# A two-layer decode kernel: one step per K slot, 18 instead of 20 slots kept, and wider loads of V

## The chip, the cores and the metric

The kernel runs on one core of one Trainium2 chip. The metric is the device time of one execution in microseconds. Every execution does the whole computation, with all inputs in HBM at the start and the result in HBM at the end. The core has five engines with instruction queues of their own: TensorE (matrix multiplies and transposes into PSUM), VectorE, ScalarE, GpSimd and SyncE. Here SyncE issues every load. An engine runs its instructions in order; order between engines is made with semaphores.

## The reference

Two identical rounds of attention and MLP follow each other, with the same weights and the same caches in both. In bfloat16, with 8 batches, 32 query heads, 8 cache heads, 8192 cached positions and a head size of 128:

```python
x = A_x                                      # [8, 1, 512]
x = x + attention(layernorm(x))              # A_k_cache, A_v_cache, A_wq, A_wo
x = x + silu(layernorm(x) @ w1) @ w2
x = x + attention(layernorm(x))
x = x + silu(layernorm(x) @ w1) @ w2

# attention, per batch and cache head (4 query heads share one):
scores = q @ K.T * 128 ** -0.5               # K [8192, 128]
o = softmax(scores) @ V                      # V [8192, 128]; then o of all heads @ wo
```

One K cache head is 2 MB, and so is one V cache head. There are 64 pairs of a batch and a cache head, and each pair is needed in both layers: 268 MB of cache, which would be 537 MB if everything were loaded twice.

## The kernel before

**Tasks and slots.** A task is one pair of batch and cache head in one layer; there are 128 (`make_tasks`, line 147). K and V of a task are split into four granules of 512 KB. SBUF has an arena of 28 slots (`NSLOT`) of one granule each: 128 partitions of 4 KB. `KEEP = 20` says that the last 20 of a batch's 32 K granules are kept: they are loaded and transposed in layer 0 and stay in fixed slots until layer 1 of that batch has used them, so that layer 1 does not load or transpose them again. The other 8 slots, and kept slots between two uses, take the loads that stream through. Tasks come in rounds: five tasks of layer 0 whose K will be kept, then some five tasks that stream K, then five of layer 1 on kept K, and so on for the eight batches.

**Positions.** The program is written out by a loop over positions `p` (line 830). A position is half a granule (1024 cache rows); a task has eight. At an odd position a slot is complete. What is emitted at a position, in this order, is:

- the query block of the next task (`emit_q`), once a task;
- the transposes up to position `p + LT` with `LT = 2` (`emit_t`, line 503): eight 128x128 transposes of K by TensorE into one of three PSUM banks, and one copy back into the same place of the slot, on ScalarE for three of eight halves (`ACT_EVAC`, line 518) and on VectorE for the others (line 520);
- at odd `p`, the scores of the slot (`emit_s`, line 537, four matmuls of 512 columns), which need both copies of this slot, and then PV of the two positions that lie `LP = 12` behind (`emit_pv`, line 605, 16 matmuls);
- a stage of the softmax of the task before (`soft`, line 817): the maximum at position 0 of the next task, the shift (two passes of an f32 matmul, line 564, with two small VectorE operations) and the exponential on ScalarE (line 576) at position 1, the sums at 3, the transposes of P (line 592) at 4, the reciprocal at 7;
- a piece of the chain between the layers, if one is due: output projection (line 711), layer norm, MLP and the next query (line 693), cut into some two dozen pieces, one a position. VectorE and GpSimd do the layer norm (lines 639 to 682);
- `issue_until(p)` (line 473): the loads whose slot comes free at this position.

So the copies of a slot have a whole step (two positions) before its scores read them: while TensorE does scores and PV of one slot, the next one is already transposed.

**Loads.** `plan_loads` (line 188) decides before the program is written which load goes into which slot. Each load has a position `need` (for K: `i0 - LT`, where its transposes are emitted) and `after`, the last position that reads what lay in the slot. Loads are taken in the order of `need` and issued in that order by SyncE, one queue for all of them. For each load the planner takes the slot with the longest lead up to `ENOUGH`, by a clock with assumed times per position (`PACE`). V is tried four granules wide, then two, then one, and a width is taken where the lead by that clock is at least `EARLIEST`; streamed K is loaded one granule at a time, kept K four at a time.

Of the kernel before, what the change touches and what calls it, by code (L numbers as in the profile page):

```python
# [14 lines left out]
GPT = 8  # L15
GPG = 2
NSLOT = 28
KEEP = 20
LT = 2
PRE = 10  # L20
KWIDE = 1
VWIDE = 4
EARLIEST = {1: 0.0, 2: 9.0, 4: 14.0}
ENOUGH = 10.0
AHEAD = 10.0
PACE = (1.24, 0.64)
LP = 12
# [9 lines left out]
PVN = 12  # L37
CW = 32
SETTLE = 1
ACT_EVAC = (1, 4, 7)  # L40

BF16 = mybir.dt.bfloat16
FP32 = mybir.dt.float32
# [144 lines left out]
def plan_loads(tasks, kept, nslot, ngran):  # L188

    at = {t: i for i, t in enumerate(tasks)}  # L190
    homes = make_homes(kept, nslot, ngran)
    clock = [0.0]
    for layer, _b, g in tasks:
        for i in range(GPT):
            clock.append(clock[-1] + PACE[int(layer == 1 and (g, i // GPG) in kept)])
    clock += [clock[-1] + PACE[0] * (n + 1) for n in range(LP + GPT)]

    heap = []

    def push(kind, i, ks, home=None):  # L200
        layer, b, g = tasks[i]
        i0 = i * GPT + ks[0] * GPG
        if kind == "K":
            need = -1 if i0 < PRE else i0 - LT
            end = i if home is None else at[(1, b, g)]
            free = [end * GPT + (k + 1) * GPG - 1 for k in ks]
        else:
            need = i0 + GPG - 1 + LP
            free = [i * GPT + (k + 1) * GPG - 1 + LP for k in ks]
        heapq.heappush(heap, (need, kind, i, ks, Load(kind, i, b, g, ks, need, free, home)))  # L210

    def split(ks, width):
        return [ks[n:n + width] for n in range(0, len(ks), width)]

    reserved = [[] for _ in range(nslot)]
    for i, (layer, b, g) in enumerate(tasks):
        if layer == 0 and g in homes:
            ks, slot = homes[g]
            push("K", i, ks, slot)
            for n in range(len(ks)):  # L220
                reserved[slot + n].append(i * GPT + ks[0] * GPG - LT)
        for ks in split([k for k in range(ngran) if (g, k) not in kept], KWIDE):
            push("K", i, tuple(ks))
        for ks in split(list(range(ngran)), VWIDE):
            push("V", i, tuple(ks))

    def lead(need, after):
        return clock[max(0, need)] - clock[after] if after >= 0 else FAR

    free = [-2] * nslot  # L230
    loads = []
    while heap:
        d = heapq.heappop(heap)[-1]
        n = len(d.ks)
        if d.home is not None:
            for m in range(n):
                reserved[d.home + m].pop(0)
        else:
            best = None
            for slot in range(nslot - n + 1):  # L240
                held = free[slot:slot + n]
                if any(r and lead(r[0], f) < AHEAD for r, f in zip(reserved[slot:slot + n], d.free)):
                    continue
                after = max(held)
                waste = sum(clock[max(0, after)] - clock[max(0, f)] for f in held)
                key = (-min(lead(d.need, after), ENOUGH), waste, -after, slot)
                best = key if best is None else min(best, key)
            if n > 1 and (best is None or -best[0] < EARLIEST[n]):
                push(d.kind, d.task, d.ks[:n // 2])
                push(d.kind, d.task, d.ks[n // 2:])  # L250
                continue
            d.slot = best[-1]
        d.after = max(free[d.slot:d.slot + n])
        assert d.after < d.need or d.need == -1 and d.after == -2, (d.kind, d.need, d.after)
        free[d.slot:d.slot + n] = d.free
        loads.append(d)
    return loads

# [17 lines left out]
def _build(ctx, nc, A_x, A_k_cache, A_v_cache, A_wq, A_wo, B_w1, B_w2, out):  # L276
# [13 lines left out]
    kept = set(order[len(order) - KEEP:])  # L290
    tasks = make_tasks(B, HKV, (len(order) - KEEP) // NGRAN)
    assert len(tasks) == 2 * B * HKV
    task_at = {t: i for i, t in enumerate(tasks)}
    loads = plan_loads(tasks, kept, NSLOT, NGRAN)
    NG = len(tasks) * GPT
# [144 lines left out]
    with nc.Block() as block:  # L440

        @block.sync
        def _(sync_eng):
# [45 lines left out]
            load_rest()  # L489

            evacs = [0]
            tevacs = [0]
            tnext = [0]

            def has_t(i):
# [7 lines left out]
            def emit_t(i):  # L503
                b, g, k, h = where(i)
                slot = k_slot[(b, g, k)]
                n = tevacs[0]
                tevacs[0] += 1
                tb = evacs[0] % NTP
                evacs[0] += 1
                tpv = TPp[tb][:, :].rearrange("p (k q) -> p k q", q=128)  # L510
                steps = [
                    lambda c=c: pe.transpose(tpv[:, c, :], chunk(slot, h * GRP + c), ident[:, :])  # L512
                    for c in range(GRP)
                ]
                mm_group(steps, reads=[r_half(slot, h), "ident"], writes=[f"TP{tb}"])
                dst = half(slot, h)
                if n % 8 in ACT_EVAC:
                    op(act, lambda: act.copy(dst, TPp[tb][:, :]), reads=[f"TP{tb}"], writes=[r_half(slot, h)])  # L518
                else:
                    op(dve, lambda: dve.tensor_copy(dst, TPp[tb][:, :]), reads=[f"TP{tb}"], writes=[r_half(slot, h)])  # L520

            def emit_t_until(i):
                while tnext[0] <= min(i, NG - 1):
                    if has_t(tnext[0]):
                        emit_t(tnext[0])
                    tnext[0] += 1
# [10 lines left out]
            def emit_s(i):  # L537
                ti = i // GPT
                b, g, k, _h = where(i)
                slot = k_slot[(b, g, k)]  # L540
                bank, qn = ti % NSCP, ti % NQB
                steps = [
                    lambda c=c: pe.matmul(  # L543
                        SCp[bank][c * QUAD:(c + 1) * QUAD, :], QB[qn][:, NGRAN - 1 - k:NGRAN - 1 - k + QUAD],
                        ARENA[:, slot * SLOT + c * KB:slot * SLOT + (c + 1) * KB],
                        start=(k == 0), stop=(k == NGRAN - 1),
                    )
                    for c in range(NQ)
                ]
                mm_group(steps, reads=[r_half(slot, 0), r_half(slot, 1), f"QB{qn}"], writes=[f"SC{bank}"])  # L550
# [279 lines left out]
            for p in range(NG + LP + GPT + 1):  # L830
                tq = (p + LQ) // GPT
                if (p + LQ) % GPT == 0 and tq < ntask:
                    layer, b, _g = tasks[tq]
                    if layer == 1 and chain and chain_b[0] == b:
                        while chain:
                            chain.pop(0)()
                    emit_q(tq)
                emit_t_until(p + LT)
                if p % GPG == GPG - 1:
                    if p < NG:  # L840
                        emit_s(p)
                    for i in range(p - LP - GPG + 1, p - LP + 1):
                        if 0 <= i < NG:
                            emit_pv(i)
                ti, ph = p // GPT - 1, p % GPT
                if 0 <= ti < ntask and ph in soft:
                    for f in soft[ph]:
                        f(ti)
                if chain:
                    left = max(1, first1[chain_b[0]] - EARLY - p)  # L850
                    late = len(chain) <= QPARTS or len(chain) > left + QPARTS // 2
                    for _n in range(2 if late and len(chain) > left else 1):
                        chain.pop(0)()
                elif heads[turn[0]] and (p >= NG or turn[0] == B
                                         or p % GPG == GPG - 1 and (tasks[p // GPT][2], 0) in kept):
                    add_heads(turn[0])
                done = p - LP - GPT
                if done >= 0 and done % GPT == 0 and done // GPT < ntask:
                    tj = done // GPT
                    emit_norm(tj)  # L860
                    layer, b, _g = tasks[tj]
                    if layer == 0:
                        heads[b].append(_g)
                    elif b == B - 1:
                        heads[B].append(_g)
                    if layer == 0 and tj == last0[b]:
                        assert not chain and turn[0] == b
                        chain.extend([lambda b=b: add_heads(b)] * (HKV - summed[b]) + chain_of(b))
                        chain_b[0] = b
                        turn[0] = b + 1  # L870
                issue_until(p)
# [48 lines left out]
```

## Time and profile before

| | before |
|---|---|
| runs, median | 1208.91 us |
| runs, lowest to highest | 1202.98 to 1213.16 us |
| profiled execution: time, span | 1205.91 us, 1204.2 us |
| TensorE busy, weight loads busy | 975.9 us, 766.5 us |
| VectorE, ScalarE, GpSimd busy | 597.2, 374.0, 70.6 us |
| read from HBM, mean rate over the span | 465.05 MB, 386 GB/s |
| loads of V: 1 MB, 512 KB | 128, 256 |
| loads of K: 2 MB, 512 KB | 40, 192 |
| copies after the transposes: VectorE, ScalarE | 440 of 690 ns, 264 of 1009 ns |

Busy time is the time in which an engine had an instruction of the program running. The span runs from the first to the last instruction; the time of an execution is a little longer. A row of the timeline gives the start in us from the span's start, the duration in us, the engine, the line of the kernel, the operation and its operands (target, then sources); a bracket at its end is the engine's idle time before it and what ended that. The granted clock is the share of TensorE's full clock that the hardware let through.

### The profile page before, as it was taken

What the parts mean: (1) busy time and instruction counts of PE and PEld (TensorE: products, weight loads), DVE (VectorE), ACT (ScalarE), POOL (GpSimd) and SP (SyncE); (2) the same over time, 40 slices, a digit from 0 to 9 for tenths busy, and PEclk for the clock granted to TensorE, in tenths of its full rate; (3) what the DMA queues carried; (4) which work ended last, traced back from release to release, by engine and by line L of the source; (5) the groups of instructions that cost most, each with busy time, mean ns of one, the idle gap of its engine ahead of it and who ended that gap; (6) DMA issues with size and microseconds to landing.
All of it is one profiled execution on the core that took longest, in us unless ns stands there. A gap on an engine that the chain in (4) does not pass through costs nothing. (4 is left out here: it accounts for less than half of the span.)

```text
span 1204.2 us, 44647 instructions
## 1 busy us (share of the span) xinstructions
PE 975.9 (81%) x19960; PEld 766.5 (64%) x19960; DVE 597.2 (50%) x1830; ACT 374.0 (31%) x658; POOL 70.6 (6%) x172
## 2 busy tenths in 40 slices
PE   2788797888878897888878897888878887888885
PEld 2566675766656675677667675677566665767564
DVE  2345553556445553556445553556445544556444
ACT  1234331333133321443223322333133322333231
POOL 0000000000000000000000000000000000000000
PEclk9789999999999998999989998999989999999996
DMA  9999999999999999999999999999999999999994
GB/s 346 398 423 400 377 377 418 422 379 377 389 422 405 383 364 423 421 383 376 410 422 388 380 371 421 422 351 366 411 422 383 377 366 422 419 376 381 399 412 161
DMA packets 95903, 467.94 MB, mean 389 GB/s; under 512 B 9936, under 2 KB 15840, under 8 KB 73696
## 3 DMA queue, kind: packets, MB, share of 16 engines
q1 hardware_dynamic: 95712, 465.10, 97.7%
q8 instruction: 156, 2.56, 0.8%
q14 instruction: 35, 0.29, 0.1%
HBM read 465.05 MB, written 0.01 MB: 386 GB/s over the span
## 5 line engine op out<-in xcount | busy, mean ns | idle before, releaser
L520 DVE COPY arena<-TPp 128x1024 bf16<-128x1024 bf16 x440 | 303.4, 690 | 410.0 <-PE TPp L512 409.8
L512 PE MATMUL TPp<-ident,arena 128*128 128x128 bf16 x5632 | 412.7, 225 | 105.2 <-DMA arena<-in_A_k_cache_dram 88.3
L512 PEld LDWEIGHTS TPp<-ident,arena 128*128 128x128 bf16 x5632 | 342.4, 101 | 118.8 <-DMA arena<-in_A_k_cache_dram 98.3
L518 ACT COPY arena<-TPp 128x1024 bf16<-128x1024 bf16 x264 | 266.4, 1009 | 308.5 <-PE TPp L512 308.5
L616 PEld LDWEIGHTS OTp<-PT,arena 128*128 128x128 bf16 x8192 | 246.7, 97 | 169.3 <-issue 130.8
L616 PE MATMUL OTp<-PT,arena 128*128 128x48 bf16 x8192 | 301.6, 185 | 43.2 <-DMA arena<-in_A_v_cache_dram 16.8
L576 ACT ACTIVATE P<-SCp,small 128x512 bf16<-128x512 f32 x128 | 87.9, 687 | 467.7 <-DVE small L572 284.8
L543 PE MATMUL SCp<-arena,QB 128*32 128x512 bf16 x2048 | 210.7, 402 | 2.9 <-ACT QB L535 1.6
L584 POOL PARTITION_ALL_REDUCE small<-small x128 | 55.7, 435 | 947.1 <-DVE small L582 919.7
L554 DVE TENSOR_REDUCE small<-SCp 128x1 f32<-128x512 f32 x128 | 87.6, 684 | 39.9 <-PE SCp L543 39.5
L543 PEld LDWEIGHTS SCp<-arena,QB 128*32 128x32 bf16 x2048 | 53.1, 93 | 51.0 <-issue 5.1
L592 PE MATMUL TPp<-ident,P 128*128 128x128 bf16 x512 | 51.0, 223 | 33.1 <-ACT P L576 22.6
L564 PE MATMUL OTp<-P,small 128*128 128x64 f32 x256 | 54.4, 294 | 22.9 <-DVE P L556 22.2
L592 PEld LDWEIGHTS TPp<-ident,P 128*128 128x128 bf16 x512 | 30.8, 98 | 45.2 <-ACT P L576 26.6
L564 PEld LDWEIGHTS OTp<-P,small 128*128 128x128 f32 x256 | 38.3, 188 | 30.5 <-DVE P L556 28.9
L567 DVE SCALAR_TENSOR_TENSOR P<-OTp,small 128x64 f32<-128x64 f32 x128 | 36.3, 284 | 42.2 <-PE OTp L564 41.4
L582 DVE TENSOR_SCALAR small<-small 128x4 f32<-128x4 f32 x128 | 28.6, 223 | 36.7 <-ACT P L576 36.7
L596 DVE COPY PT<-TPp 128x256 bf16<-128x256 bf16 x128 | 36.9, 288 | 10.0 <-PE TPp L592 10.0
L711 PE MATMUL MISC<-at,wo 128*128 128x32 bf16 (+1 forms) x1152 | 39.8, 175 | 0.3 <-DVE at L630 0.3
L693 PE MATMUL MISC<-small,wq 128*128 128x32 bf16 x1024 | 35.0, 177 | 1.2 <-issue 1.2
L711 PEld LDWEIGHTS MISC<-at,wo 128*128 128x128 bf16 x1152 | 35.0, 96 | 0.4 <-DVE at L630 0.4
L556 DVE TENSOR_SCALAR P<-ident,small 128x64 f32<-128x64 bf16 x128 | 32.6, 254 | 4.5
(59 smaller groups left out, 300.4 us busy)
## 6 DMA issues: line engine op xcount, KB each, us to landing
arena<-in_A_v_cache_dram SPq DMA_DIRECT2D x128, 1024.0 KB, 10.4
arena<-in_A_v_cache_dram SPq DMA_DIRECT2D x256, 512.0 KB, 7.1
arena<-in_A_k_cache_dram SPq DMA_DIRECT2D x192, 512.0 KB, 7.7
arena<-in_A_k_cache_dram SPq DMA_DIRECT2D x40, 2048.0 KB, 14.7
wq<-in_A_wq_dram SPq DMA_DIRECT2D x1, 4096.0 KB, 16.8
wo<-in_A_wo_dram SPq DMA_DIRECT2D x1, 4096.0 KB, 29.6
w<-in_B_w_dram SPq DMA_DIRECT2D x2, 1792.0 KB, 25.2
P<-in_A_x_dram SPq DMA_DIRECT2D x1, 8.0 KB
```

Source lines behind the costliest of these rows:

```text
L512: lambda c=c: pe.transpose(tpv[:, c, :], chunk(slot, h * GRP + c), ident[:, :])
L518: op(act, lambda: act.copy(dst, TPp[tb][:, :]), reads=[f"TP{tb}"], writes=[r_half(slot, h)])
L520: op(dve, lambda: dve.tensor_copy(dst, TPp[tb][:, :]), reads=[f"TP{tb}"], writes=[r_half(slot, h)])
L543: lambda c=c: pe.matmul(SCp[bank][c * QUAD:(c + 1) * QUAD, :], QB[qn][:, NGRAN - 1 - k:NGRAN - 1 - k + QUAD], ARENA[:, slot * SLOT + c * K ...
L554: op(dve, lambda: dve.tensor_reduce(rowmax, SCp[bank][:, :], AX.X, ALU.max), reads=[f"SC{bank}"], writes=["rowmax"])
L564: mm_group([lambda: pe.matmul(every, ones.to_broadcast([128, 128]), spread, start=True, stop=True)], reads=["ones", "P"], writes=[f"OT{ob}"])
L576: op(act, lambda: act.activation(P[:, :], SCp[bank][:, :], ACT.Exp, bias=shift, scale=SM_SCALE, accum_out=rs[st]), reads=[f"SC{bank}", "sh ...
L584: op(pool, lambda: pool.partition_all_reduce(ssa[st], ssm[st], 128, bass.bass_isa.ReduceOp.add), reads=[f"ssm{st}"], writes=[f"ssa{st}"])
L592: lambda c=c: pe.transpose(tpv[:, c, :], P[:, c * 128:(c + 1) * 128], ident[:, :])
L596: op(dve, lambda: dve.tensor_copy(PT.rearrange("p x (c q) -> p x c q", q=USED), tpv.rearrange("p x (c q) -> p x c q", q=QUAD)[:, :, :, 0:U ...
L616: lambda c=c, cc=cc: pe.matmul(otp, chunk(slot, h * GRP + c), pv[:, cc % CPB, cc // CPB % NQ, k, :].unsqueeze(2).to_broadcast([128, REP, P ...
L711: lambda o=o, h=h: pe.matmul(MISC[:, o * w:(o + 1) * w], wo_sb[:, h, o * 128:(o + 1) * 128], rhs_of(h).to_broadcast([128, w]) if n == 1 el ...
```

## The change

- `KEEP` goes from 20 to 18: two K granules of one cache head per batch are no longer kept, so ten slots are left for streaming.
- `LT` is gone. At an odd position the transposes of both halves of the slot are emitted, then PV, then the scores of the same slot. A K load's `need` becomes the odd position of its slot.
- `ACT_EVAC` is gone: the first half of each slot is copied by ScalarE, the second by VectorE.
- The planner asks for more lead before it takes a double (12 instead of 9) or fourfold (16 instead of 14) load, counts lead up to 16 instead of 10, and, between slots that are otherwise equal, takes the one that held V last.

The loads become 240 single, 70 double and 33 fourfold for V, and 224 single, 8 double and 32 fourfold for K.

```diff
-KEEP = 20
-LT = 2
+KEEP = 18
...
-EARLIEST = {1: 0.0, 2: 9.0, 4: 14.0}
-ENOUGH = 10.0
+EARLIEST = {1: 0.0, 2: 12.0, 4: 16.0}
+ENOUGH = 16.0
...
-ACT_EVAC = (1, 4, 7)
...
-            need = -1 if i0 < PRE else i0 - LT
+            need = -1 if i0 < PRE else i0 + GPG - 1
...
-                reserved[slot + n].append(i * GPT + ks[0] * GPG - LT)
+                reserved[slot + n].append(i * GPT + (ks[0] + 1) * GPG - 1)
...
+    keys = [0] * nslot
...
-                key = (-min(lead(d.need, after), ENOUGH), waste, -after, slot)
+                key = (-min(lead(d.need, after), ENOUGH), waste, -after, sum(keys[slot:slot + n]), slot)
...
+        keys[d.slot:d.slot + n] = [int(d.kind == "K")] * n
...
-                if n % 8 in ACT_EVAC:
+                if h == 0:
                     op(act, lambda: act.copy(dst, TPp[tb][:, :]), reads=[f"TP{tb}"], writes=[r_half(slot, h)])
                 else:
                     op(dve, lambda: dve.tensor_copy(dst, TPp[tb][:, :]), reads=[f"TP{tb}"], writes=[r_half(slot, h)])
...
-                emit_t_until(p + LT)
                 if p % GPG == GPG - 1:
-                    if p < NG:
-                        emit_s(p)
+                    emit_t_until(p)
                     for i in range(p - LP - GPG + 1, p - LP + 1):
                         if 0 <= i < NG:
                             emit_pv(i)
+                    if p < NG:
+                        emit_s(p)
```

## The prediction

> **What bounds the kernel now.** I read the page first, then the waits, then single steps in the timeline.
>
> ```profile
> span 1204.2 us, 44647 instructions
> ...
> q1 hardware_dynamic: 95712, 465.10, 97.7%
> ```
> ```profile
> PE TPp L512 <- DMA arena<-in_A_k_cache_dram: 88.3, 85, 5.3
> ...
> PE OTp L616 <- DMA arena<-in_A_v_cache_dram: 16.8, 32, 1.4
> ```
>
> The first fence is from the page (span; the load queue's packets, MB and share), the second from the list of waits (us in total, times, longest). The load queue is busy for 97.7% of the span, so the loads look like the bound. But TensorE waited only 88.3 + 16.8 = 105 us for them, and the DMA share cannot separate the two: in windows of 30 us it is 1.01 where 421 GB/s move (480 to 510 us) and 0.99 where 374 GB/s move (540 to 570 us). I therefore asked how long a task (one cache head, four K slots) takes where nothing waits for a load. The exponential comes once per task, so the distance between two of them is a task's time.
>
> ```profile
> 262.93 0.69 ACT L576 ACTIVATE P<-SCp,small 128x512 bf16<-128x512 f32 x1 [3.00 <-DVE small L572]
> ...
> 271.30 0.69 ACT L576 ACTIVATE P<-SCp,small 128x512 bf16<-128x512 f32 x1 [3.00 <-DVE small L572]
> ```
>
> A task that transposes its K takes 8.37 us without load waits (262.93 to 271.30), 8.76 with one output-projection piece (254.17 to 262.93); a task on kept K takes about 4.9 (191.37 to 196.31). Tasks beside the MLP chain repeat 11.99 us in round after round (548.64 to 560.63). Loads at the best windows' 422 GB/s would need 4.19 MB / 422 = 9.9 us for a transposing task. So the two bounds are close: TensorE has 1.5 us of slack per transposing task, and that is what the change spends.
>
> ```profile
> 372.41 1.07 PE L512 MATMUL TPp<-ident,arena 128*128 128x128 bf16 x16 [0.93 <-DMA arena<-in_A_k_cache_dram]
> 373.07 0.69 DVE L520 COPY arena<-TPp 128x1024 bf16<-128x1024 bf16 x1 [2.87 <-PE TPp L512]
> 373.40 0.10 PEld L543 LDWEIGHTS SCp<-arena,QB 128*32 128x32 bf16 x4
> 373.41 0.40 PE L543 MATMUL SCp<-arena,QB 128*32 128x512 bf16 x4
> 373.51 1.01 ACT L518 COPY arena<-TPp 128x1024 bf16<-128x1024 bf16 x1 [2.12 <-PE TPp L512]
> ...
> 373.74 0.57 PE L616 MATMUL OTp<-PT,arena 128*128 128x48 bf16 x16
> ...
> 374.15 1.05 PE L512 MATMUL TPp<-ident,arena 128*128 128x128 bf16 x16
> ...
> 376.71 1.06 PE L512 MATMUL TPp<-ident,arena 128*128 128x128 bf16 x16
> ...
> 377.53 0.69 ACT L576 ACTIVATE P<-SCp,small 128x512 bf16<-128x512 f32 x1 [3.00 <-DVE small L572]
> ...
> 378.21 1.00 ACT L518 COPY arena<-TPp 128x1024 bf16<-128x1024 bf16 x1
> ```
>
> These are rows of the timeline (start, duration, engine, line). A step now is: transposes of the next slot (16 in 0.99 us to the next start), scores of the slot transposed a step earlier (0.33), PV (0.41): 1.73 us, nothing waiting. The copy of the first half starts 0.66 us after the transposes do, that of the second half at 1.10. In the third block the ScalarE copy starts only at 1.50, since the exponential stands ahead of it.
>
> **The change, part by part.**
>
> *Order within the step (LT gone, scores after PV).* The scores now need the copies of the transposes issued just before. First half on ScalarE: 0.66 + 1.01 = 1.67. Second half on VectorE: 1.10 + 0.69 = 1.79, plus 0.06 from a copy's end to TensorE: scores start at 1.85. PV covers only to 0.99 + 0.41 = 1.40. The step is 1.85 + 0.33 = 2.18 us. One step in four is worse: softmax_shift is emitted at the end of the task's first step, so its exponential is ahead of the next step's first-half copy on ScalarE; copy 1.50 to 2.50, scores at 2.56, step 2.89. With the two f32 matmuls of the shift (0.27) and the four transposes of P (0.23), a task is 3 x 2.18 + 2.89 + 0.50 = 9.93 us; the waits at L564 and L592 (0.39 and 0.22 a task) go, since transposes and PV now stand before them. Against 8.37: +1.56 on 88 tasks, **+137 us**. In the order of the built program 24 exponential steps have a chain or projection piece (16, 28 or 32 matmuls) before the transposes, which shortens the stall by 0.4 to 0.7: -12.
>
> *Tasks on kept K.* PV now precedes the scores, so the scores' 0.33 no longer covers the wait for PT: 32 tasks x 0.33 = +11.
>
> *KEEP 20 to 18.* Two slots a batch are loaded and transposed again in layer 1: 16 loads of 0.524 MB, 256 transposes, 32 copies. The eight tasks concerned go from 4.9 us to two stalled steps (2.18 + 0.27, 2.89) and two short ones (1.5 with the wait for PT, 0.7), 7.6: +22. The 8.4 MB at the mean 389 GB/s are 21.6 us of queue; I cost them at nothing, because the queue (473.5 MB, 1122 us at 422 GB/s) is then the shorter of the two, and keep the 21.6 as a rival.
>
> *ACT_EVAC gone.* ScalarE copies 368 halves instead of 264: +105 us busy, to some 479; VectorE loses 72 x 0.69 = 50. Both stay under half the span; their cost is in the steps above.
>
> *Layer-norm pieces.* Their chains (6 and 7 VectorE operations of some 0.19 us) sit ahead of the second-half copy. By counting through the new order I get about 2.4 us per batch against 1.31 now (a PV wait behind VectorE, once a round): +9, bounds 0 and +19.
>
> *Loads.* The plan asks for a slot ten positions (five steps) ahead of use instead of six or seven positions, from ten streaming slots instead of eight; V goes as 240 single, 70 double and 33 fourfold loads. TensorE being slower by 1.5 us a task, most of the 105 us of load waits go, and with them the slow clock behind the long ones:
>
> ```profile
> 208.07 1.89 PE L512 MATMUL TPp<-ident,arena 128*128 128x128 bf16 x16 [3.63 <-DMA arena<-in_A_k_cache_dram]
> ```
>
> Sixteen transposes took 1.89 us after that gap, 1.05 elsewhere; with the next block (1.81) and the scores some 2 us, eight times, 17. Of 122 I leave 26 standing: 9 at the start, where a fourfold V load and a third K load now go out ahead of the 7.9 MB of weights (2.6 MB, 6.5 us later for the K behind them), the rest where both bounds meet. Gain -96; bounds -122 and -40.
>
> Sum: 137 - 12 + 11 + 22 + 9 - 96 = +71. Span 1204.2 + 71 = 1275; the profiled execution took 1205.91, 1.7 more than its span, and 3.0 less than the median shown. I say **1276 us**. About 1% is what a measurement here tells from no change (the runs shown lie 0.8% apart).
>
> [...]
>
> **The rivals.**
>
> 1. *The queue stays the bound and hides the stalls* (for: 97.7%; a transposing task needs 9.9 us of loads anyway; against: 8.76 us tasks in the kept stage, 11.99 us tasks that no load explains). The cost is then the added bytes: 1204 + 21.6, **1227** us. Chance 0.10.
> 2. *Faster: the queue never runs dry.* With five steps of loads outstanding, everything moves at 422 GB/s: 1122 us, and about 27 for the edges (the last slice of 30 us moves 161 GB/s, the first 346), **1150**. It decides if transposing steps take under 2.48 us on average including the chain's pieces; against it stands that the copies' 1.85 us come from rows, and that PV is too short to cover them. Chance 0.08.
> 3. *They cancel:* the stalls cost half of what I count, the load waits go: about 1205. Chance 0.04.
> 4. *The clock falls.* Each transposing step now has a gap of 0.45 or 1.16 us. Gaps of 0.9 left the granted clock at 1.00 (510 to 540 us); a window behind a 3.6 us gap had 0.89 (600 to 630). At 0.89 throughout, 88 tasks of 7.4 us of matmul work take about 80 us more: **1355**. Chance 0.04. The Trainium skill (TensorE: Matmul & The Clock Gate, A second HAM failure mode) describes such an oscillation from short repeated gaps; no row here shows it.
>
> **How the numbers follow.** The forecast, 1235 to 1315 by its bounds, has 0.74. Range 1222 to 1312: it takes in rival 1 and leaves out 2, 3 and 4 and some of the upper end. Faster by over 1%: rival 2, 0.08; within 1%: 0.04; slower: 0.88.
>
> **What would show it.** Right: in a warm step the scores start 1.85 us after the transposes, 2.56 in the step with the exponential; idle time before the scores' matmuls (2.9 us now) becomes 150 to 220 us, ended by the copies; transposing tasks take 9.9 to 10.4 us; load waits at the transposes fall under 40 us; ScalarE is busy some 480 us. The eight long gaps before the first kept K go. Wrong: if the wait for K stays near 88 us, the queue still binds (rival 1); if the DMA rate stays above 410 GB/s in all stages, rival 2; if PEclk stands at 9 in most slices, rival 4. The term I trust least is the 26 us of load waits left.

## The result, and the profile after

The changed kernel takes 1300.49 us (median of 4 runs, 1298.46 to 1305.68), the kernel before 1211.04 us on the same chip: a ratio of 1.0758, 95% interval 1.0697 to 1.0819. The profiled execution took 1300.67 us with a span of 1298.8. The forecast was 1276 us, in a range of 1222 to 1312.

From the page of the kernel after: the span, the busy time of the engines, and the load queue with packets, MB and share.

```profile
span 1298.8 us, 45667 instructions
...
PE 978.0 (75%) x20216; PEld 801.4 (62%) x20216; DVE 574.2 (44%) x1758; ACT 478.2 (37%) x762; POOL 70.9 (5%) x172
...
q1 hardware_dynamic: 94416, 473.49, 94.2%
```

TensorE's matmuls are busy for 978.0 us, close to the 975.9 before. So nearly all of the 95 us that the span has gained are idle time of TensorE. The load queue still shows 94.2%, but its rate has fallen from 386 to 365 GB/s read. The list of waits of the kernel after (us in total, times, longest) says what TensorE waits for now:

```profile
PE SCp L540 <- DVE arena L517: 80.7, 173, 0.9
PE SCp L540 <- ACT arena L515: 73.2, 70, 1.1
PE SCp L540 <- DVE small L600: 33.5, 71, 0.5
...
PE TPp L509 <- DMA arena<-in_A_k_cache_dram: 7.4, 3, 6.4
```

The wait of the transposes for K has gone from 88.3 to 7.4 us, that of PV for V has left the list, and the scores' matmuls, which had 2.9 us of idle time in all, now have 229.1. These are their lines on the page, before and after (behind the second bar: the idle time before them, and what ended most of it):

```profile
L543 PE MATMUL SCp<-arena,QB 128*32 128x512 bf16 x2048 | 210.7, 402 | 2.9 <-ACT QB L535 1.6
```
```profile
L540 PE MATMUL SCp<-arena,QB 128*32 128x512 bf16 x2048 | 213.9, 406 | 229.1 <-DVE arena L517 80.7
```

(L600 in the list of waits is a small VectorE instruction that is emitted behind the copy; the scores read nothing of it and wait for the copy.) A transposing task without a projection piece, from one exponential to the next, in the timeline:

```profile
380.01 0.69 ACT L573 ACTIVATE P<-SCp,small 128x512 bf16<-128x512 f32 x1 [1.65 <-DVE small L569]
...
390.17 0.69 ACT L573 ACTIVATE P<-SCp,small 128x512 bf16<-128x512 f32 x1 [1.65 <-DVE small L569]
```

It takes 10.16 us, task after task, against 8.37 before (10.56 against 8.76 with a projection piece). And the steps themselves, first the one with the exponential, then one without:

```profile
410.52 1.06 PE L509 MATMUL TPp<-ident,arena 128*128 128x128 bf16 x16
...
411.29 0.69 ACT L573 ACTIVATE P<-SCp,small 128x512 bf16<-128x512 f32 x1 [1.65 <-DVE small L569]
411.41 0.56 PE L613 MATMUL OTp<-PT,arena 128*128 128x48 bf16 x16
411.61 0.69 DVE L517 COPY arena<-TPp 128x1024 bf16<-128x1024 bf16 x1 [0.35 <-PE TPp L509]
...
411.97 1.00 ACT L515 COPY arena<-TPp 128x1024 bf16<-128x1024 bf16 x1
...
413.02 0.40 PE L540 MATMUL SCp<-arena,QB 128*32 128x512 bf16 x4 [1.05 <-ACT arena L515]
...
416.27 1.05 PE L509 MATMUL TPp<-ident,arena 128*128 128x128 bf16 x16
416.91 1.01 ACT L515 COPY arena<-TPp 128x1024 bf16<-128x1024 bf16 x1 [1.56 <-PE TPp L509]
417.16 0.56 PE L613 MATMUL OTp<-PT,arena 128*128 128x48 bf16 x16
417.36 0.69 DVE L517 COPY arena<-TPp 128x1024 bf16<-128x1024 bf16 x1 [1.99 <-PE TPp L509]
...
418.20 0.40 PE L540 MATMUL SCp<-arena,QB 128*32 128x512 bf16 x4 [0.47 <-DVE small L600]
```

Transposes, PV, a gap, scores. With the exponential the scores start 2.51 us after the transposes (median of 70 such steps), right behind ScalarE's copy (411.97 + 1.00, and 0.05). Without it they start 1.93 us after them, though the last copy ends at 418.05: 0.15 us lie between its end and the scores. The prediction had 0.06 there, in every step.

### The profile page after: what moved, and what is told of

It reads as the page before. It is cut to its first block, busy times and chain, and to the rows that moved or that the text cites. A ratio compares the mean times of both kernels' runs of the same rounds, so it can differ in the third digit from the quotient of the medians.

```text
span 1298.8 us, 45667 instructions
## 1 busy us (share of the span) xinstructions
PE 978.0 (75%) x20216; PEld 801.4 (62%) x20216; DVE 574.2 (44%) x1758; ACT 478.2 (37%) x762; POOL 70.9 (5%) x172
## 3 DMA queue, kind: packets, MB, share of 16 engines
q1 hardware_dynamic: 94416, 473.49, 94.2%
## 5 line engine op out<-in xcount | busy, mean ns | idle before, releaser
L515 ACT COPY arena<-TPp 128x1024 bf16<-128x1024 bf16 x368 | 371.6, 1010 | 437.3 <-PE TPp L509 437.1
L509 PE MATMUL TPp<-ident,arena 128*128 128x128 bf16 x5888 | 405.5, 224 | 20.7 <-DVE arena L517 11.3
L509 PEld LDWEIGHTS TPp<-ident,arena 128*128 128x128 bf16 x5888 | 355.3, 101 | 50.6 <-issue 41.2
L540 PE MATMUL SCp<-arena,QB 128*32 128x512 bf16 x2048 | 213.9, 406 | 229.1 <-DVE arena L517 80.7
L517 DVE COPY arena<-TPp 128x1024 bf16<-128x1024 bf16 x368 | 254.4, 692 | 277.1 <-PE TPp L509 276.5
L613 PE MATMUL OTp<-PT,arena 128*128 128x48 bf16 x8192 | 298.3, 185 | 21.2 <-DVE at L627 14.7
L613 PEld LDWEIGHTS OTp<-PT,arena 128*128 128x128 bf16 x8192 | 265.6, 98 | 44.8 <-issue 44.5
L540 PEld LDWEIGHTS SCp<-arena,QB 128*32 128x32 bf16 x2048 | 61.6, 94 | 267.9 <-ACT arena L515 194.3
L564 DVE SCALAR_TENSOR_TENSOR P<-OTp,small 128x64 f32<-128x64 f32 x128 | 36.3, 284 | 109.7 <-PE OTp L561 109.7
L589 PE MATMUL TPp<-ident,P 128*128 128x128 bf16 x512 | 52.1, 226 | 19.3 <-ACT P L573 19.3
L561 PEld LDWEIGHTS OTp<-P,small 128*128 128x128 f32 x256 | 38.7, 190 | 39.6 <-issue 22.0
L561 PE MATMUL OTp<-P,small 128*128 128x64 f32 x256 | 56.5, 303 | 7.6 <-DVE P L553 7.6
L589 PEld LDWEIGHTS TPp<-ident,P 128*128 128x128 bf16 x512 | 29.8, 99 | 47.7 <-ACT P L573 27.2
L690 PEld LDWEIGHTS MISC<-small,wq 128*128 128x128 bf16 x1024 | 29.5, 96 | 7.2 <-issue 7.2
```

The source lines that it names most:

```text
L540: lambda c=c: pe.matmul(SCp[bank][c * QUAD:(c + 1) * QUAD, :], QB[qn][:, NGRAN - 1 - k:NGRAN - 1 - k + QUAD], ARENA[:, slot * SLOT + c * K ...
L561: mm_group([lambda: pe.matmul(every, ones.to_broadcast([128, 128]), spread, start=True, stop=True)], reads=["ones", "P"], writes=[f"OT{ob}"])
L589: lambda c=c: pe.transpose(tpv[:, c, :], P[:, c * 128:(c + 1) * 128], ident[:, :])
L613: lambda c=c, cc=cc: pe.matmul(otp, chunk(slot, h * GRP + c), pv[:, cc % CPB, cc // CPB % NQ, k, :].unsqueeze(2).to_broadcast([128, REP, P ...
```

## The experiments

### Where the time goes: the order of the step alone, and all but the order

`order_back` keeps every part of the change (18 kept, the copies by half, the planner's limits) but the order of the step. `order_alone` is the kernel before with the new order and nothing else.

```diff
 order_back, against after
+                emit_t_until(p + LT)
                 if p % GPG == GPG - 1:
-                    emit_t_until(p)
+                    if p < NG:
+                        emit_s(p)
                     for i in range(p - LP - GPG + 1, p - LP + 1):
                         if 0 <= i < NG:
                             emit_pv(i)
-                    if p < NG:
-                        emit_s(p)
```

(With it, K's `need` is `i0 - LT` again; `order_alone` makes the opposite edits in the kernel before. As `need` moves, the planner, itself unchanged, arrives at a somewhat different plan: in `order_alone` V goes as 202 single and 155 double loads.)

> The changed kernel with one part undone: transposes again two positions ahead, scores before PV, need of a K load as before. 18 slots kept, the planner's new limits and the copies by half stay. Step theory (the scores now wait for the copies of the same step, and that is the loss): idle time before the scores falls from 229 us to under 15, transposing tasks fall from 10.2 to 8.4 to 9.9 us, the time to 1185 to 1230. Rival, queue theory (8.4 MB more and the new sizes of loads are the loss): the time stays above 1270.

> The kernel before with the new order alone: transposes, PV, scores in one step. 20 slots kept, the old planner, the old copies (three of eight halves on ScalarE, so three slots of four have their last copy later than in the changed kernel, by some 0.2 us). Step theory: transposing tasks of 10.2 to 11.2 us, 1275 to 1330. Queue theory: the bytes are those of before, so 1200 to 1225.

Measured: `order_back` 1204.44 us, ratio 0.9936 (0.9913 to 0.9959); `order_alone` 1308.10 us, ratio 1.0800 (1.0758 to 1.0841). The waits of `order_back`:

```profile
PE TPp L510 <- DMA arena<-in_A_k_cache_dram: 97.8, 69, 10.8
...
PE OTp L614 <- DMA arena<-in_A_v_cache_dram: 13.4, 19, 3.3
```

and those of `order_alone`:

```profile
PE SCp L543 <- ACT arena L518: 127.9, 166, 1.2
PE SCp L543 <- DVE arena L520: 98.6, 164, 2.6
...
PE TPp L512 <- DMA arena<-in_A_k_cache_dram: 6.4, 3, 4.4
```

The two lists have changed places. (The fastest transposing tasks of `order_back` take 7.75 us, less than the 8.4 expected; the copies by half do that, as shown below.) With the old order TensorE waits for loads as before, whatever the planner and the slots; with the new order it waits for the copies, and the loads are mostly early though there are only eight streaming slots and the old planner (PV still waits 10.7 us for V there, against 16.8 before). So the order is the whole loss, and it also is what takes the load waits away: not because loads come earlier, but because TensorE comes later. The other parts together are worth 0.6% in the other direction.

### How long TensorE takes where no load is late

`half_v_after` and `half_v_before` leave out half of V's bytes (every load of V after the first into its slot brings only the first half of each granule) and keep the instructions of the engines.

```diff
+        if d.kind == "V" and all(d.slot + m in filled for m in range(n)):
+            src = src.rearrange("p (m c) -> p m c", c=SLOT)[:, :, 0:SLOT // 2]
+            dst = dst.rearrange("p (m c) -> p m c", c=SLOT)[:, :, 0:SLOT // 2]
+        filled.update(range(d.slot, d.slot + n))
```

> The changed kernel, which leaves out half of V's bytes: every load of V after the first into its slot brings only the first half of each granule, so some 130 of 473 MB are not loaded; all instructions of the engines stay. Step theory: TensorE's own pace binds, transposing tasks stay at 10.2 and 10.6 us, the time at 1280 to 1300. Queue theory: the time falls under 1200, by up to the 130 MB / 367 GB/s = 350 us.

> The kernel before, which leaves out half of V's bytes in the same way. This measures how much of its time is waiting for loads. Step theory: TensorE's pace comes to light, transposing tasks of 8.4 to 8.8 us throughout, the 105 us of load waits and the slow clock behind them go, 1080 to 1110. Queue theory: 335 MB at 389 GB/s are 860 us, so the time falls under 1050.

The page of `half_v_after`, and then that of `half_v_before`:

```profile
span 1293.3 us, 45667 instructions
...
q1 hardware_dynamic: 114512, 343.46, 77.0%
```
```profile
span 1090.3 us, 44647 instructions
...
q1 hardware_dynamic: 111072, 335.08, 86.1%
```

The times are 1295.10 and 1092.07 us, both where the step theory put them. Taking away 130 MB of loads saves the kernel after 1298.8 - 1293.3 = 5.5 us and the kernel before 1204.2 - 1090.3 = 113.9 us. Each is one run, and four runs of the kernel after lie 7 us apart: the 113.9 stands far out of that, the 5.5 says only that little is left. This splits the result as the prediction's sum did: TensorE's own pace became 1293.3 - 1090.3 = 203 us longer, and 113.9 - 5.5 = 108 us of load waits went. The net is 95, as in the two profiled executions (1298.8 - 1204.2). The split is good to some 10 us, for a few load waits are left in both kernels (first `half_v_before`, then `half_v_after`):

```profile
PE TPp L517 <- DMA arena<-in_A_k_cache_dram: 18.0, 16, 5.8
```
```profile
PE TPp L514 <- DMA arena<-in_A_k_cache_dram: 10.7, 2, 10.3
```

### Two terms of the step: the exponential ahead of the copy, and the hand-off to the scores

In `exp_late` the exponential is emitted two positions later, behind the next step's copies.

```diff
-            soft = {0: [softmax_max], 1: [softmax_shift, softmax_exp], 3: [softmax_sum], 4: [emit_pt], 7: [softmax_rcp]}
+            soft = {0: [softmax_max], 1: [softmax_shift], 3: [softmax_exp, softmax_sum], 4: [emit_pt], 7: [softmax_rcp]}
```

> The changed kernel with the exponential emitted after the transposes, PV and scores of position 3 instead of at position 1, so that on ScalarE it stands behind the copy of that step and not ahead of it. Step theory: the scores of that step start 1.93 us after the transposes, as in the other steps, instead of 2.50; the exponential then ends some 2.4 us after them and the transposes of P wait some 0.15; a transposing task falls from 10.16 to 9.7 to 9.8 us, the time to 1260 to 1275. Rival: the later exponential makes the transposes of P and PV late by as much as the scores gain, 1292 to 1305.

Measured: 1280.21 us (1275.31 to 1289.08), ratio 1.0559 (1.0503 to 1.0615). Nearly all transposing steps (321 of 368) now have their scores 1.93 us after the transposes, those with the exponential too, and a task takes 9.71 us, 0.45 less than in after: the mechanism holds. The time missed the expected range by 5 us. Two things that took part of the gain back are seen in the trace: the step that a chain piece had shortened is no longer shortened (in after 326.1 - 314.2 = 11.9 us for such a task, here 12.7), and loads are late again in some tasks (waits for K 18.2 instead of 7.4 us).

Next, the 0.15 us behind the copy. In the trace of after it is 146 ns in 292 steps in which VectorE's copy ends last, and 53 ns in 70 steps with the exponential, in which ScalarE's does. TensorE has two waits there, first for ScalarE's copy, then for VectorE's. `swap_waits` emits them in the other order and changes nothing else.

```diff
-                mm_group(steps, reads=[r_half(slot, 0), r_half(slot, 1), f"QB{qn}"], writes=[f"SC{bank}"])
+                mm_group(steps, reads=[r_half(slot, 1), r_half(slot, 0), f"QB{qn}"], writes=[f"SC{bank}"])
```

> The kernel after with one edit: the scores' two waits are emitted in the other order, first for VectorE's copy (which ends last in the steps without the exponential), then for ScalarE's. In the trace of after the scores follow the end of the last copy by 146 ns where the copy waited for second ends last (295 steps), and by 53 ns where the copy waited for first does (69 steps with the exponential). Theory, that the order of the two waits makes the difference: 146 falls to some 55 ns in the steps without the exponential and rises to some 146 in those with it, the scores of a plain step start 1.84 us after its transposes (the 1.85 of the prediction), a transposing task takes 9.95 to 10.0 us, and the time is about 1283 us. Rival, that the 146 ns belong to VectorE's end, whatever the order of the waits: the scores stay at 1.93, tasks at 10.16, and the time at 1300.

From the timeline of `swap_waits`, a step without the exponential:

```profile
413.35 1.05 PE L509 MATMUL TPp<-ident,arena 128*128 128x128 bf16 x16
414.00 1.01 ACT L515 COPY arena<-TPp 128x1024 bf16<-128x1024 bf16 x1 [1.47 <-PE TPp L509]
414.44 0.69 DVE L517 COPY arena<-TPp 128x1024 bf16<-128x1024 bf16 x1 [1.89 <-PE TPp L509]
...
415.19 0.40 PE L540 MATMUL SCp<-arena,QB 128*32 128x512 bf16 x4 [0.38 <-DVE arena L517]
```

The copy ends at 415.13, the scores follow after 55 ns (279 of the 299 steps in which VectorE's copy is last), 1.85 us after the transposes. With the exponential, where ScalarE's copy is last, it is now 145 ns (68 of 69 steps). The two numbers have changed sides with the order of the waits, so the engine that ends last is not the cause. A task takes 9.98 us instead of 10.16. The time is 1294.18 us (1288.92 to 1301.43), ratio 1.0693 (1.0627 to 1.0759); its interval overlaps that of after, so the gain of 0.18 us a task is shown by the steps and not by the times of the runs. The median is 11 us above the 1283 expected, the profiled execution (1290.31) 7.

`exp_late_swap` has both edits.

> The kernel after with both edits: the exponential two positions later (as in exp_late) and the scores' two waits in the other order (as in swap_waits). All 368 hand-offs then have VectorE's copy last and waited for first: scores 1.85 us after the transposes in every step, a transposing task 9.35 to 9.4 us. Theory, that TensorE's order alone sets the time: 365 steps by 0.09 us are 33 us less than exp_late's 1280, 1247 us, with load waits at the transposes near exp_late's 18 us. Rival, that the load queue takes its bound back as soon as a transposing task falls under the 9.9 us that its 4.19 MB need at 422 GB/s: load waits at the transposes rise to over 35 us and the time is 1255 to 1270 us, still slower than before.

Measured: 1262.48 us (1258.89 to 1264.62), ratio 1.0425 (1.0390 to 1.0460). From its timeline, the step with the exponential:

```profile
411.74 1.06 PE L509 MATMUL TPp<-ident,arena 128*128 128x128 bf16 x16
413.30 0.69 ACT L573 ACTIVATE P<-SCp,small 128x512 bf16<-128x512 f32 x1
413.58 0.40 PE L540 MATMUL SCp<-arena,QB 128*32 128x512 bf16 x4 [0.38 <-DVE arena L517]
414.13 0.40 PE L589 MATMUL TPp<-ident,P 128*128 128x128 bf16 x4 [0.16 <-ACT P L573]
```

The scores start 1.84 us after the transposes in 316 of 368 steps, and a task takes 9.44 us. Neither theory is wholly right. The time lies in the rival's range, but its reason is absent: the waits for K are 18.8 us, as in `exp_late`. The span fell by 15 us (1274.4 to 1259.4) instead of 33. Of the rest, some 10 are the wait for P at L589, 0.16 us in the last row (19.7 us in all in `exp_late`, 30.0 here), and 7 are tasks on kept K, which ran at a slower clock (204.7 us for the 32 of them there, 212.1 here; the last section has the rows). With both stalls shortened, the new order is still 4% slower than the kernel before.

### The other parts in the old order

Five kernels keep the old order and vary what is left. The first three start from `order_back`.

```diff
 back_keep20, against order_back
-KEEP = 18
+KEEP = 20
 back_old_copies, against order_back
-                if h == 0:
+                if n % 8 in ACT_EVAC:
 back_old_plan, against order_back
-EARLIEST = {1: 0.0, 2: 12.0, 4: 16.0}
-ENOUGH = 16.0
+EARLIEST = {1: 0.0, 2: 9.0, 4: 14.0}
+ENOUGH = 10.0
-                key = (-min(lead(d.need, after), ENOUGH), waste, -after, sum(keys[slot:slot + n]), slot)
+                key = (-min(lead(d.need, after), ENOUGH), waste, -after, slot)
 copies_alone, against before
-                if n % 8 in ACT_EVAC:
+                if h == 0:
 keep16, against back_old_plan
-KEEP = 18
+KEEP = 16
```

> The run order_back (1204.4 us) with 20 slots kept again, so that of the change the planner's limits and the copies by half stay. Queue theory for this order (load queue at 97.6%): 8.4 MB less at 394 GB/s are 21 us, 1180 to 1190. Rival: the two streaming slots that go cost in waits what the bytes save, 1200 to 1215.

> The run order_back with the old division of the copies (three of eight halves on ScalarE). The fastest transposing tasks go from 7.75 us back to 8.37. If the load queue binds wherever no chain runs, 1204 to 1212; if TensorE's pace binds, 88 times 0.6 us more, 1230 to 1255.

> The run order_back with the planner's old limits and tie break, so V goes as 158 single and 177 double loads instead of 248 single, 70 double and 31 fourfold. If the sizes and leads of loads matter, slower, 1215 to 1235; if not, 1198 to 1210.

> The kernel before with one edit: the first half of each slot is copied by ScalarE, the second by VectorE. Theory, that the order of the steps is the whole cost and that the copies by half are worth a few us in the old order (back_old_copies against order_back, 5 us): 1202 to 1210 us, and a transposing task without load waits some 7.8 instead of 8.4 us, since the exponential's copies no longer fall in an uneven pattern. Rival, that ScalarE, with a copy in every step, is late for the exponential: tasks over 8.4 us, 1220 us.

> The old order of a step and the old planner, copies by half, and two more slots for streaming (16 kept, 12 streaming) than in back_old_plan: 8 MB more to load and 16 more slots to transpose. If streaming slots are still worth more than their bytes (20 to 18 kept was worth 8 us with the other planner): 1195 to 1200 us. If the queue's bytes decide by now (8.4 MB at some 400 GB/s are 21 us): 1215 to 1225 us.

| kernel | kept | planner | copies | us, median | ratio, 95% interval |
|---|---|---|---|---|---|
| order_back | 18 | new | by half | 1204.44 | 0.9936 (0.9913 to 0.9959) |
| back_keep20 | 20 | new | by half | 1212.47 | 1.0003 (0.9971 to 1.0035) |
| back_old_copies | 18 | new | old | 1209.52 | 0.9975 (0.9955 to 0.9995) |
| back_old_plan | 18 | old | by half | 1203.83 | 0.9915 (0.9884 to 0.9947) |
| copies_alone | 20 | old | by half | 1201.99 | 0.9921 (0.9891 to 0.9950) |
| keep16 | 16 | old | by half | 1207.64 | 0.9987 (0.9962 to 1.0012) |

The copies by half are worth 0.4% with the new planner and 18 kept (0.9936 against 0.9975; the two intervals touch) and 0.8% alone, which is all that any of these kernels gains. In the old order a transposing task without load waits falls from 8.37 to 7.75 us with them: the wait at L564, 22.2 us in all before, is gone. In the profiled execution of `copies_alone` most of that came back as load waits, for K (103.6 us, 88.3 before) and for V (19.5, 16.8 before). The new limits of the planner cost 0.8% with 20 kept (`back_keep20` against `copies_alone`) and nothing with 18. Keeping 18 instead of 20 is worth 8 us only with the new limits; with the old ones (`copies_alone`, `back_old_plan`) the two are equal. Read alone, `order_back` against `back_keep20` would have credited the two streaming slots with those 8 us. `back_keep20` lies in its rival's range: 8.4 MB less to load gained nothing. `keep16` came out between its two expectations. `copies_alone` and `back_old_plan` are both faster than the kernel before, by 0.8%, and much faster than after.

## Why the prediction was right, and which terms were off

**The likeliest case happened, by its mechanism.** The bound moved from the load queue to TensorE's order, and the step's end is set by the copies. The time, 1300, lies 24 us above the forecast and inside the range. Nearly all that the prediction asked to see is there: idle time before the scores 229 us, ended by the copies (150 to 220 were named, so it is slightly over); transposing tasks 10.16 us, and 10.56 with a projection piece (9.9 to 10.4 named); load waits at the transposes 7.4 us (under 40); ScalarE busy 478.2 us (some 480); no long gap before a kept K is left. The bounds of its terms, added up, reach from about 1241 to 1342 us, not from 1235 to 1315 as it says; 1300 lies inside either.

**Term by term**, on the split that the halved loads give (203 us of pace, 108 of load waits; the prediction had 167 and 96):

- *Transposing tasks, +137.* Measured 10.16 - 8.37 = 1.79 us on 88 tasks, 158 us. This is the term that was mis-sized most, by 20 us. The step that failed is "plus 0.06 from a copy's end to TensorE": it is 0.15 in a plain step. The kernel before has 0.06 where TensorE waits for one engine (at L564 behind VectorE, 58 times of 59); the new step waits for two, and the one that is last is waited for second. Without these 0.09 us in the three plain steps a task of 10.16 us would take 9.89, against 9.93 in the working: the rest of the sum was right.
- *Tasks on kept K, +11.* Measured 5.62 - 4.86 = 0.76 us on 32 tasks, 24 us. The prediction counted one longer wait, that for PT (L613): 0.47 instead of 0.14, its 0.33 to the hundredth. Two more got longer. The rows of after:

```profile
205.63 0.25 DVE L553 TENSOR_SCALAR P<-ident,small 128x64 f32<-128x64 bf16 x1
205.94 0.43 PE L561 MATMUL OTp<-P,small 128*128 128x64 f32 x2 [0.25 <-DVE P L553]
...
207.87 0.40 PE L589 MATMUL TPp<-ident,P 128*128 128x128 bf16 x4 [0.76 <-ACT P L573]
...
208.74 0.56 PE L613 MATMUL OTp<-PT,arena 128*128 128x48 bf16 x16 [0.47 <-DVE at L627]
```

And the same places before:

```profile
192.20 0.40 PE L592 MATMUL TPp<-ident,P 128*128 128x128 bf16 x4 [0.66 <-ACT P L576]
...
193.07 0.65 PE L616 MATMUL OTp<-PT,arena 128*128 128x48 bf16 x16
...
195.24 0.41 PE L564 MATMUL OTp<-P,small 128*128 128x64 f32 x2
```

With the scores at the end of the step, PV no longer stands between them and the shift, which waits 0.25 us for the maximum and what VectorE makes of it (L561, no wait before); the exponential is waited for longer too (L589, 0.76 instead of 0.66). The three make 0.68 of the 0.76 us. The prediction asked of the moved scores only what they had covered, not who reads them.
- *Chain pieces, KEEP and layer norm, -12 + 22 + 9 = 19.* Together 203 - 158 - 24 = 21 us. That the sum is right is luck. In the traces of `half_v_after` and `half_v_before`, counted from one exponential to the next, the eight tasks that KEEP concerns take 6.85 us each, not the 7.6 of the working, and together 54.8 against 41.9 us: 13, not 22. The 84 transposing tasks behind the first four take 934.4 against 765.3 us, 169 more, of which 84 x 1.79 = 150 are the steps. So the chain pieces and the layer norm, put at -12 + 9, cost some 19, give or take the load waits that are left; these runs do not part the two. In the layer norm's step, once a round, the scores waited 2.14 us instead of 1.05 (VectorE's second-half copy starts only at 301.48, behind its chain). In four of the eight rounds the matmuls behind that gap ran slowly, which the prediction had not counted; here is one:

```profile
302.31 0.52 PE L540 MATMUL SCp<-arena,QB 128*32 128x512 bf16 x4 [2.14 <-DVE small L579]
...
303.17 1.91 PE L509 MATMUL TPp<-ident,arena 128*128 128x128 bf16 x16
```

- *Loads, -96.* Measured -108. Of the 26 us left standing 5.5 remained; the 9 us feared at the start did not come (the fourth exponential starts at 80.9 us in both kernels). The reason given, wider lead and ten slots, was not needed for K: `order_alone`, with neither, waits 6.4 us for it. It does wait 10.7 us for V, and after does not, so they may be worth that.

So the load term was 12 us too careful, the cost of pace 36 us too small, and the forecast 24 too low; the two errors made up for each other in part.

**The rivals.** The queue as a bound (1227) is refuted by `half_v_after`: 130 MB fewer, 5.5 us. The faster case needed transposing steps under 2.48 us on average, the chain's pieces included; they take 2.79 (the 84 transposing tasks behind the first four: 935.9 us for 336 steps). The cancelling one needed half the stall; it is longer than counted. The clock did not fall in the transposing tasks: the granted clock is 0.97 and 0.98 (100 to 200 and 400 to 500 us), with a gap of 0.47 or 1.05 us in every step. The sign named for that case, PEclk (the granted clock on the page, in tenths, by slices) at 9 in most slices, could not tell: a 9 there stands for anything from 0.9 up, and most slices of the kernel before have it too (mean granted clock 0.957 before, 0.959 after). The Trainium skill (TensorE: Matmul & The Clock Gate, A second HAM failure mode) describes a clock that oscillates from short idle times between groups of matmuls; the transposing tasks here do not agree with it (343 of the 368 groups of sixteen transposes take 1.05 to 1.18 us), the tasks on kept K do in part (rows in the last section).

The share of weight loads would have misled. It fell from 64% to 62% while TensorE's order became the bound. The Trainium skill (Perfetto Trace Analysis, Identifying the Most-Contended Engine) names that share, beside the matmul work done against peak, as the measure of TensorE's headroom; here it says nothing of an engine that stands in order behind two copies, and the queue's 94.2% says the opposite of what `half_v_after` shows.

## What to carry to other kernels

Before an instruction is moved next to its producer, add up the path through the other engine (here 0.66 + 1.01, and 1.10 + 0.69 us) and compare it with the work that stays between them (1.40): what is missing is paid in every step, and the busy shares of engines and queue will not show it. When a kernel has two bounds close together, make one of them cheap (shorter loads, same instructions) and time the other alone; the difference of two such runs takes in what the list of waits leaves out (here 113.9 us against the 105 listed). Where an instruction waits for two engines, emit first the wait that ends last (here 0.09 us each time).

## What the runs showed of the hardware that was not expected

- **The order of two waits.** From the end of the last copy to the first matmul of the scores: 146 ns where that copy is waited for second, 53 to 55 ns where it is waited for first and the other is long past. Seen from both sides in after (292 and 70 steps) and, turned round, in `swap_waits` (68 and 279); `exp_late` has 145 to 148 in 360 of its 368 steps, `exp_late_swap` 54 to 56 in 357. In `order_alone`, steps with a single wait have 55 (87 steps), and nearly all others (253 of 264), in which now ScalarE's and now VectorE's copy is last and waited for second, 144 to 146. What the engine does in these 90 ns no trace shows.
- **A slow clock without a long gap.** In tasks on kept K the same waits (0.76 us before the transposes of P, 0.47 before PV) are followed by full speed in one task and by a slow stretch in another. First a slow stretch of some 3 us behind such a wait in `exp_late_swap`, then the last kept tasks of after, where the granted clock is 0.55 from 1225 to 1248 us with no gap over 0.76 us between the matmuls:

```profile
348.87 0.80 PE L613 MATMUL OTp<-PT,arena 128*128 128x48 bf16 x16 [0.47 <-DVE at L627]
349.60 0.62 PE L540 MATMUL SCp<-arena,QB 128*32 128x512 bf16 x4
...
352.14 0.40 PE L540 MATMUL SCp<-arena,QB 128*32 128x512 bf16 x4
```
```profile
1226.34 0.40 PE L589 MATMUL TPp<-ident,P 128*128 128x128 bf16 x4 [0.76 <-ACT P L573]
1227.21 0.66 PE L613 MATMUL OTp<-PT,arena 128*128 128x48 bf16 x16 [0.48 <-DVE at L627]
1227.80 0.62 PE L540 MATMUL SCp<-arena,QB 128*32 128x512 bf16 x4
```

  Four matmuls of the scores take 0.62 instead of 0.40 us, and a kept task then 6.5 or more instead of 5.62. The longer gaps of 1.05 us, once in each transposing task, did not do this, and behind the eight gaps of 2.14 us at the layer norm the transposes ran slowly in four rounds and not in the others. What decides stays open; the length of the last gap alone does not.
- **Wide loads.** The planners of `order_back` and `back_old_plan` load V in different widths (70 double and 31 fourfold loads against 177 double ones) at the same bytes, and the times are equal (1204.44 and 1203.83 us).
